# Second mixture: logits with x as the weights, a hand-written beginning with operands split from PSUM, and attention's first projection moved up

## The chip, the cores and the metric

The kernel runs on 1 core of a Trainium2 chip. The metric is the device time of one execution in microseconds (us); lower is better. The engines are PE (TensorE: matmuls, and PEld, its weight loads), DVE (VectorE), ACT (ScalarE), POOL (GpSimd) and SP (SyncE, which here issues nearly all DMAs).

## What is computed

Three stages follow one another: an attention with exponential features, a mixture of experts with one expert per token, and a second mixture in which all eight experts work on every token, weighted by a gate matrix that eight Sinkhorn-like steps balance. Everything is float32; 2304 tokens of 512 features, 8 experts of 1024 hidden units.

```python
def _attn_ref(q, k, v, w_phi):
    def phi(x):
        proj = np.einsum('bhsd,df->bhsf', x, w_phi)
        proj = proj - np.max(np.abs(proj), axis=-1, keepdims=True)
        return np.concatenate([np.exp(proj), np.exp(-proj)], axis=-1)
    ...

def _moe2_ref(x, w_gate, w1, w2):
    N, D = x.shape
    E = w_gate.shape[1]
    logits = x @ w_gate
    logits = logits - logits.max()
    P = np.exp(logits)
    for _ in range(8):
        P /= P.sum(1, keepdims=True) + 1e-09
        P /= P.sum(0, keepdims=True) + 1e-09
        P *= N / E
    out = np.zeros((N, D), dtype=np.float32)
    for e in range(E):
        h = np.maximum(x @ w1[e], 0.0)
        ye = h @ w2[e]
        out += P[:, e:e + 1] * ye
    return out
```

## The kernel before

**Attention** (`attention`, L39) runs through steps of four 128-token halves. A step has `transp` (L112: four PE transposes into one PSUM tile, copied by ACT to `th`), `proj` (L131: 8 matmuls of fp32, two row halves side by side, into the one PSUM buffer `pp`), `center` (L141: two DVE operations of 1024 columns that read `pp`) and `expo` (L148: two ACT operations). The order on PE, DVE and ACT is written out by hand (`manual_schedule`, L299); SP and POOL are left to the planner. `busy(n)` (L295) puts n transposes of the identity on PE, whose result nobody reads. At the start the order on PE is: 9 of these, the transposes of step 0, 8 more, the transposes of step 1, the projection of step 0, 16 more, and then step 1's projection.

**The first mixture** (`moe1`) ends with a scatter of its last rows to `x2d` in DRAM.

**The second mixture** (`moe2`, L816) takes the tokens in 3 passes of 2 x 384 (`h` is which 384, `TB` = 3 tiles of 128 each) and each expert's hidden units in quads of 512. Both matmuls of a quad are Strassen-like, with seven products (`mm`, L1115) instead of eight; an operand of a product is 128 x 2 x 384 (`xcb[1..7]`), as a high part (rounded to the matmul's format, by ACT, `x_high`) and a low part (the rest, by DVE, `x_low`); a product is six matmuls, high by high, high by low and low by high. Operands 1 and 2 are raw blocks of x, 6, 7, 5, 3 and 4 are sums or raw blocks (`sum_x`, `sum_4`, on DVE here). `group` (L1167) runs the seven products of 128 hidden units: `a` (PSUM `pa`) from products 1 and 2, `b` (`pb`) from 6, 5 and 3, `d` (`pd`) from 7 and 4. The copies `s`, `v`, `z` of these sums are ACT's. The `fill` functions put other work between the products: for quad 0 the transposes, the storing and the logits of the other two passes' tokens (`other_logits`, L960, four calls), later the second matmul of the quad before (`piece`).

The first three quads and all that stands before them are not written out in order. The planner takes instructions by their order in the program and by when its own model has their inputs and engine ready; in a `manual_schedule` region an engine's instructions keep the order of the program among themselves, while instructions from outside may come between. From quad 3 on everything is by hand.

The beginning (L1222 to L1245): six x tiles of 128 tokens are loaded by SP (`load_x`), each transposed on PE (four transposes into one PSUM tile, L943), and copied to `xq`, whole blocks by ACT and DVE in turn (`x_block`, L984). The operands 1 and 2 are then split from `xq`. In `group` of quad 0 the pieces `lead` stand between the two halves of `a`: `x_logits(0)`, `finish_a`, `x_logits(1)`.

`logits` (L947) has the gate weights `wg` (128 x 8 per block of 128 features) as the stationary operand and streams 384 tokens, four fp32 matmuls into an 8 x 384 tile; ACT copies that to `gt`, which has the one buffer of tag "v" in common with the copy `v`; three transposes bring 128 x 8 blocks to PSUM, and DVE copies them to `lg`. An fp32 matmul stands in the trace as two records. When all six calls are done, `sinkhorn_start` and the steps follow, in quads 0 to 2, and at their end `store_gates`.

PSUM tags: "pa" 1 buffer, "pb" 2, "pd" 1, "Y" 2, "T" 2.

Of the kernel before, what the change touches and what calls it, by code (L numbers as in the profile page):

```python
# [7 lines left out]
F32 = mybir.dt.float32  # L8
# [30 lines left out]
def attention(tc, nc, cp, q, k, v, w_phi, w_gate, w_skip, lgs, routed, stepped, early, last_steps):  # L39
# [3 lines left out]
    with ExitStack() as ctx:  # L43
# [251 lines left out]
        def busy(n):  # L295
            for _ in range(n):
                nc.tensor.transpose(warm, ident, ident)

        with tc.manual_schedule(engines={nc.tensor.engine, nc.vector.engine, nc.scalar.engine}):  # L299
            busy(9)  # L300
            th = transp(steps[0])
            busy(8)
            for g in range(len(steps) + 1):
                cur = steps[g] if g < len(steps) else []
                if cur:
                    if g:
                        t = center(proj(th))
                    else:
                        nth = transp(steps[1])
                        t = center(proj(th))  # L310
                        th = nth
                        busy(16)
                    if 0 < g < len(steps) - 1:
                        th = transp(steps[g + 1])
                    if g == 1:
                        busy(8)
# [499 lines left out]
def moe2(tc, nc, c, w_gate, w1, w2, x2d, xtd, wd1, wd2, ptd, out):  # L816
# [6 lines left out]
    with ExitStack() as ctx:  # L823
# [97 lines left out]
        def acc0(i):  # L921
            return Z[:, D * i : D * i + D]
# [16 lines left out]
        def transposed(xr, dst, copy=lambda d, s: nc.scalar.activation(d, s, AF.Copy)):  # L939

            pt = ps.tile([P, NKB, P], F32, name="pt", tag="T", bufs=2)
            for kb in range(NKB):
                nc.tensor.transpose(pt[:, kb], xr[:, kb * P : kb * P + P], c["ident"])  # L943
            for d, s in dst(pt):
                copy(d, s)

        def logits(ps_, h, src):  # L947

            pg = ps.tile([E, TW], F32, name="pg", tag="T", bufs=2)
            for kb in range(NKB):  # L950
                nc.tensor.matmul(pg, wg[:, kb], src(kb), start=(kb == 0), stop=(kb == NKB - 1))
            gt = big.tile([E, TW], F32, name="gt", tag="v")
            nc.scalar.activation(gt, pg, AF.Copy)
            pl = ps.tile([P, TB, E], F32, name="pl", tag="T", bufs=2)
            for i in range(TB):
                nc.tensor.transpose(pl[:, i], gt[:, i * P : i * P + P], c["ident"][0:E, 0:E])
            t = tiles(ps_, h)[0]
            nc.vector.tensor_copy(lg[:, t : t + TB], pl)

# [21 lines left out]
                for kh in range(2):  # L981
                    xq[h, kh] = new_xq()

        def x_block(xr, h, i):  # L984
            sl = slice(i * P, i * P + P)
            to = lambda pt: [(xq[h, kh][:, :, sl], pt[:, 2 * kh : 2 * kh + 2]) for kh in range(2)]
            if (h + i) % 2:
                transposed(xr, to, nc.vector.tensor_copy)
            else:
                transposed(xr, to)  # L990

        def x_logits(h):
            logits(0, h, lambda kb: xq[h, kb // 2][:, kb % 2])
# [132 lines left out]
        def copied(src, nm, tag):  # L1126
            t = big.tile([P, TW], F32, name=nm, tag=tag)
            nc.scalar.activation(t, src, AF.Copy)  # L1128
            return t
# [34 lines left out]
            if n == NW - 1:  # L1164
                nc.sync.dma_start(row(t, 1), accs[t])

        def group(n, g, fill, high, low, lead=()):  # L1167


            a, b, d = [ps.tile([P, TW], F32, name=nm, tag=nm, bufs=bf) for nm, bf in (("pa", 1), ("pb", 2), ("pd", 1))]  # L1170
            v = nc.vector
            mm(a, 1, g, True, False)
            s = copied(a, "s", "sz")

            def finish_a():
                mm(a, 2, g, False, True)
                relu_high(n, g, 0, 0, a)
                relu_low(n, g, 0, 0, a)

            if lead:  # L1180
                lead[0]()
                finish_a()
                lead[1]()
            mm(b, 6, g, True, False)
            high[0]()
            v.tensor_tensor(b, b, s, ALU.add)
# [2 lines left out]
            mm(d, 7, g, True, False)  # L1189
            high[1]()  # L1190
            low[1]()
            if not lead:
                finish_a()
            for k in (2, 3):
                high[k]()
                low[k]()
# [23 lines left out]

        none = lambda: None
        new_x()  # L1222
        xrs = [[load_x(t, acc0(TB * h + i)) for i, t in enumerate(tiles(0, h))] for h in range(2)]
        for h in range(2):
            for i, t in enumerate(tiles(0, h)):
                x_block(xrs[h][i], h, i)
            if h == 0:
                xs.update({1: xq[0, 0], 2: xq[0, 1]})
                for i in (1, 2):
                    x_high(i)  # L1230
                    x_low(i, True)
        for i in range(3):
            sum_x(i, True)
            if i:
                x_high(ORDER[i])
                x_low(ORDER[i])
        sum_4()
        for i in (5, 3, 4):
            x_high(i)
            x_low(i)  # L1240
        others = [(ps_, h) for ps_ in range(1, NPASS) for h in range(2)]
        load_w2(0, 0)
        load_w2(0, 1)
        for i in (6, 7, 5, 3):
            store_w1(0, i)  # L1245

        def both(*fs):
            def f():
# [4 lines left out]

        def quad(n):
            more = n + 1 < NW
            for g in range(2):
                high, low = [none] * 7, [none] * 7
                if n == 0:
# [37 lines left out]
                    low[k] = both(low[k], lambda i=i, g=g: sums_low(n, i, g))  # L1296
                if g:
                    low[0] = both(low[0], lambda: store_w2(n, 1))
                lead = [lambda: x_logits(0), lambda: x_logits(1)] if n == 0 and g == 0 else ()
                group(n, g, fill, high, low, lead)  # L1300
                if g and more:
                    if n + 2 < NW:
                        load_w1(n + 2)
# [382 lines left out]
```

## Time and profile before

| | us |
|---|---|
| median of 3 runs | 1936.58 |
| all runs | 1937.0, 1936.58, 1931.12 |
| the profiled execution | 1931.85 |
| its span, first to last instruction | 1930.1 |

| engine | busy share of the span |
|---|---|
| PE | 98% |
| PEld | 92% |
| DVE | 70% |
| ACT | 48% |
| POOL | 39% |

The shares are means over stages with different limits; what a change in one stage is worth is read from that stage. In a row of a timeline stand the start in us, the time from the first start to the last end, the engine (with q: its sequencer, which issues DMAs), the line, the operation, the tiles written and read, shapes, how often it stands in a row, and in brackets how long the engine was idle before it and what ended that. Matmuls overlap, so the time of a row is not its count times the time of one. The granted clock of PE is 1.00 for 2.4 GHz and 0.50 for 1.2 GHz.

### The profile page before, as it was taken

How to read it: one execution, taken by the hardware profiler on the slowest of the kernel's cores; microseconds unless marked ns; L12 is line 12 of the kernel's file. 1: busy time of each engine (PE TensorE's matmuls, PEld its weight loads, DVE VectorE, ACT ScalarE, POOL GpSimd, SP SyncE). 2: the span in 40 equal slices, each digit the busy share in tenths (PEclk: the TensorE clock that was granted, in tenths of full speed). 3: DMA queues.
4: the chain of work that ended last, by engine and by line, in shares of the span. 5: the costliest groups of instructions: out<-in, count | busy, mean ns of one | idle time of the engine just before them, and what ended most of it. 6: DMA issues, size and time to landing. Idle time of an engine off the chain costs nothing.

```text
span 1930.1 us, 34988 instructions
## 1 busy us (share of the span) xinstructions
PE 1887.2 (98%) x13028; PEld 1778.1 (92%) x13028; DVE 1343.9 (70%) x2309; ACT 930.8 (48%) x1679; POOL 745.9 (39%) x653
## 2 busy tenths in 40 slices
PE   9999999989999999999999999999999999999997
PEld 8998899956889988999899999999999999999997
DVE  5778977664967676767657766767786676676665
ACT  5778655545444444445344444444445444444442
POOL 2012522222433334333124455445563454444445
PEclk9999999999999999999999999999999999999999
DMA  7424686648766767777476676777656766767663
GB/s 196 119 66 164 221 281 220 211 136 288 250 219 243 254 246 245 256 267 269 140 256 224 229 237 217 237 241 251 228 174 232 237 218 232 234 223 246 227 201 110
DMA packets 234691, 422.00 MB, mean 219 GB/s; under 512 B 31594, under 2 KB 151374, under 8 KB 234508
## 3 DMA queue, kind: packets, MB, share of 16 engines
q1 hardware_dynamic: 230892, 412.16, 64.2%
q0 software_dynamic: 3456, 7.40, 1.1%
q8 instruction: 106, 1.74, 0.4%
q14 instruction: 77, 0.63, 0.1%
q10 hardware_dynamic: 160, 0.07, 0.0%
HBM read 311.18 MB, written 110.86 MB: 219 GB/s over the span
## 4 chain that ended last, share of the span: by engine, by line
PE 69%; DVE 3%; POOL 1%; DMA 1%; issue 0%; ACT 0%; POOLq 0%; DVEq 0%; ACTq 0%
PE pu L1359 23%; PE pb L1120 15%; PE py L1155 12%; PE pd L1120 10%; PE pa L1120 9%; POOL acc L1449 1%; POOL hr L1449 0%; DVE hh L1406 0%; DMA w<-wd 0%; DVE wc L884 0%; DVE xcl L1018 0%; DVE acc L1374 0%; DVE hr L1398 0%; DVE hh L1141 0%; DVE acc L1449 0%
## 5 line engine op out<-in xcount | busy, mean ns | idle before, releaser
L1359 PE MATMUL pu<-hh,w 128*128 128x384 f32 x2688 | 541.1, 336 | 8.4 <-DVE acc L1449 4.2
L1359 PEld LDWEIGHTS pu<-hh,w 128*128 128x128 f32 x2688 | 473.9, 188 | 9.4 <-DVE acc L1449 4.6
L1449 POOL TENSOR_TENSOR hr<-hr 128x384 f32<-128x384 f32 (+1 forms) x192 | 282.3, 1470 | 290.0 <-DVE hr L1398 167.6
L1120 PE MATMUL pb<-xch,wc 128*128 128x384 f32 x1152 | 297.7, 339 | 1.8 <-ACT v L1128 0.8
L1402 ACT ACTIVATE hh<-hr 128x384 fp32r<-128x384 f32 (+2 forms) x256 | 189.2, 761 | 204.6 <-POOL hr L1449 152.1
L1155 PE MATMUL py<-w,hh 128*128 128x512 f32 x1152 | 287.5, 396 | 0.0
L1406 DVE TENSOR_TENSOR hh<-hr,hh 128x384 fp32r<-128x384 f32 (+2 forms) x256 | 223.3, 881 | 63.9 <-ACT hh L1402 62.6
L1155 PEld LDWEIGHTS py<-w,hh 128*128 128x128 f32 x1152 | 215.4, 189 | 43.2 <-issue 1.9
L1372 POOL TENSOR_TENSOR acc<-acc,s 128x384 f32<-128x384 f32 x147 | 162.3, 1105 | 224.0 <-ACT s L1371 223.9
L1374 DVE TENSOR_TENSOR acc<-pu,acc 128x384 f32<-128x384 f32 x267 | 147.3, 553 | 103.9 <-PE pu L1359 103.0
L1120 PEld LDWEIGHTS pb<-xch,wc 128*128 128x128 f32 x1152 | 210.2, 188 | 9.7 <-ACT v L1128 1.7
L1120 PE MATMUL pa<-xch,wc 128*128 128x384 f32 x768 | 198.8, 338 | 0.1
L1120 PE MATMUL pd<-xch,wc 128*128 128x384 f32 x768 | 198.0, 338 | 0.5 <-DVE c L1213 0.5
L1371 ACT ACTIVATE s<-pu 128x384 f32<-128x384 f32 x147 | 72.1, 491 | 162.2 <-PE pu L1359 162.0
L1120 PE MATMUL pb<-xcl,wc 128*128 128x384 f32 x576 | 148.8, 339 | 0.0
L1120 PEld LDWEIGHTS pa<-xch,wc 128*128 128x128 f32 x768 | 139.8, 187 | 4.1 <-ACT acc L1102 0.6
L1120 PEld LDWEIGHTS pd<-xch,wc 128*128 128x128 f32 x768 | 140.0, 188 | 1.3 <-DVE c L1213 0.8
L884 DVE TENSOR_TENSOR wc<-r,wc 128x512 fp32r<-128x512 f32 x170 | 130.6, 769 | 3.8 <-ACT wc L881 3.4
L881 ACT ACTIVATE wc<-r 128x512 fp32r<-128x512 f32 x170 | 105.8, 623 | 10.6 <-PE pa L1120 9.2
L1120 PEld LDWEIGHTS pb<-xcl,wc 128*128 128x128 f32 x576 | 104.9, 188 | 0.0
L1120 PE MATMUL pa<-xcl,wc 128*128 128x384 f32 x384 | 99.1, 338 | 0.1
L1120 PE MATMUL pd<-xcl,wc 128*128 128x384 f32 x384 | 99.1, 339 | 0.0
(271 smaller groups left out, 2975.0 us busy)
## 6 DMA issues: line engine op xcount, KB each, us to landing
w<-wd SPq DMA_DIRECT2D x224, 512.0 KB, 4.2
wc<-wd SPq DMA_DIRECT2D x120, 512.0 KB, 4.9
r<-in_moe_w_dram SPq DMA_DIRECT2D x108, 512.0 KB, 4.9
wd<-wc SPq DMA_DIRECT2D x64, 512.0 KB, 3.7
wd<-acc SPq DMA_DIRECT2D x128, 256.0 KB, 3.0
wd<-w SPq DMA_DIRECT2D x96, 256.0 KB, 3.8
r<-in_moe_w_dram SPq DMA_DIRECT2D x90, 256.0 KB, 3.8
acc<-in_moe_w_dram SPq DMA_DIRECT2D x64, 256.0 KB, 3.6
```

What stands on the lines that cost most here:

```text
L881: nc.scalar.activation(wc[i][:, 0], wsrc[i], AF.Copy)
L884: nc.vector.tensor_tensor(wc[i][:, 1], wsrc[i], f32(wc[i][:, 0]), ALU.subtract)
L1120: nc.tensor.matmul(dst, wc[i][:, w, kb, sl], xcb[i][x][:, kb], start=(start and m == 0), stop=(stop and m == 5), skip_group_check=True,)
L1155: nc.tensor.matmul(py, ht[:, i * P : i * P + P], w[:, wt], start=(m == 0), stop=(m == 11))
L1359: nc.tensor.matmul(pu, w[:, wl, kb, g2 * P : g2 * P + P], H[:, hx[kb][xl].start + o], start=(m == 0), stop=(m == 5))
L1371: nc.scalar.activation(tmp, pu, AF.Copy)
L1372: nc.gpsimd.tensor_tensor(t, t, tmp, ALU.add)
L1374: nc.vector.tensor_tensor(t, pu, t, ALU.add)
L1402: nc.scalar.activation(H[:, hx[g][0]], R[:, u:v], AF.Copy)
L1406: nc.vector.tensor_tensor(H[:, hx[g][1]], R[:, u:v], f32(H[:, hx[g][0]]), ALU.subtract)
L1449: eng.tensor_tensor(out_, a, b, op)
```

## The change

Three things. `logits` makes the x blocks the stationary operand (128 x 128) and streams `wg` (8 columns), twelve fp32 matmuls per call, whose result is already tokens by experts: the copy `gt` and the transposes fall away. The beginning of the second mixture becomes `lead`, in a `manual_schedule` region over all engines: operands 1 and 2 are split straight from the transposes' PSUM tiles (`x_split`), the raw copies to `xq` follow (`x_raw`, one half by ACT, the other by DVE), and products, sums and logits have a written order; `load_w2` stands ahead of it in the program, the rest of the operands and `store_w1` (`rest_x`) behind it. In attention, step 0's projection moves ahead of step 1's transposes, with 4 warm transposes before each of them in place of 8.

```diff
@@ attention
             th = transp(steps[0])
-            busy(8)
+            busy(4)
...
                     else:
-                        nth = transp(steps[1])
                         t = center(proj(th))
-                        th = nth
+                        busy(4)
+                        th = transp(steps[1])
                         busy(16)
@@ logits
-            pg = ps.tile([E, TW], F32, name="pg", tag="T", bufs=2)
-            for kb in range(NKB):
-                nc.tensor.matmul(pg, wg[:, kb], src(kb), start=(kb == 0), stop=(kb == NKB - 1))
-            gt = big.tile([E, TW], F32, name="gt", tag="v")
-            nc.scalar.activation(gt, pg, AF.Copy)
             pl = ps.tile([P, TB, E], F32, name="pl", tag="T", bufs=2)
             for i in range(TB):
-                nc.tensor.transpose(pl[:, i], gt[:, i * P : i * P + P], c["ident"][0:E, 0:E])
+                for kb in range(NKB):
+                    nc.tensor.matmul(
+                        pl[:, i], src(kb)[:, i * P : i * P + P], wg[:, kb], start=(kb == 0), stop=(kb == NKB - 1)
+                    )
@@ x_block
+        def x_turn(xr, tag):
+            pt = ps.tile([P, NKB, P], F32, name="pt", tag=tag, bufs=2)
+            for kb in range(NKB):
+                nc.tensor.transpose(pt[:, kb], xr[:, kb * P : kb * P + P], c["ident"])
+            return pt
+
+        def x_split(pt, i):
             sl = slice(i * P, i * P + P)
...
+            for op, kh in ((1, 0), (2, 1)):
+                src = pt[:, 2 * kh : 2 * kh + 2]
+                dh, dl = [t[:, :, sl] for t in xcb[op]]
+                nc.scalar.activation(dh, src, AF.Copy)
+                nc.vector.tensor_tensor(dl, src, f32(dh), ALU.subtract)
+
+        def x_raw(pt, h, i):
+            sl = slice(i * P, i * P + P)
+            nc.scalar.activation(xq[h, 0][:, :, sl], pt[:, 0:2], AF.Copy)
+            nc.vector.tensor_copy(xq[h, 1][:, :, sl], pt[:, 2:4])
@@ group
+        def first_a(a, g):
+            mm(a, 1, g, True, False)
+            return copied(a, "s", "sz")
+
+        def finish_a(a, n, g):
+            mm(a, 2, g, False, True)
+            relu_high(n, g, 0, 0, a)
+            relu_low(n, g, 0, 0, a)
+
+        def group(n, g, fill, high, low, s=None):
+            a = None
...
+            if s is None:
+                a = ps.tile([P, TW], F32, name="pa", tag="pa", bufs=1)
+                s = first_a(a, g)
             mm(b, 6, g, True, False)
...
-            if not lead:
-                finish_a()
+            if a is not None:
+                finish_a(a, n, g)
@@ beginning
+        def lead():
+            xrs = [load_x(t, acc0(TB * h + i)) for h in range(2) for i, t in enumerate(tiles(0, h))]
+            pts = []
+            for i in range(TB):
+                pts.append(x_turn(xrs[i], "YYT"[i]))
+                x_split(pts[i], i)
+            a = ps.tile([P, TW], F32, name="pa", tag="pa", bufs=1)
+            for i in range(TB):
+                x_raw(pts[i], 0, i)
+            s = first_a(a, 0)
+            for i in range(TB):
+                pt = x_turn(xrs[TB + i], "YYT"[i])
+                x_raw(pt, 1, i)
+            finish_a(a, 0, 0)
+            sum_x(0, True)
+            sum_x(1, True)
+            x_high(6)
+            x_low(6)
+            x_logits(0)
+            sum_x(2, True)
+            x_high(7)
+            x_low(7)
+            x_logits(1)
+            return s
+
         others = [(ps_, h) for ps_ in range(1, NPASS) for h in range(2)]
         load_w2(0, 0)
         load_w2(0, 1)
-        for i in (6, 7, 5, 3):
-            store_w1(0, i)
+
+        def rest_x():
+            sum_4()
+            for i in (5, 3, 4):
+                x_high(i)
+                x_low(i)
+            for i in (6, 7, 5, 3):
+                store_w1(0, i)
@@ quad
+            s = None
+            if n == 0:
+                with tc.manual_schedule():
+                    s = lead()
+                rest_x()
...
-                lead = [lambda: x_logits(0), lambda: x_logits(1)] if n == 0 and g == 0 else ()
-                group(n, g, fill, high, low, lead)
+                group(n, g, fill, high, low, s if g == 0 else None)
```

## Rows read from the trace of the kernel before

**Rows 1.** The page: busy time, share of the span and instructions of PE.

```profile
PE 1887.2 (98%) x13028; PEld 1778.1 (92%) x13028; DVE 1343.9 (70%) x2309; ACT 930.8 (48%) x1679; POOL 745.9 (39%) x653
```

**Rows 2.** Windows: length, busy us (instructions) of PE, PEld, DVE, ACT, POOL, clock, DMA share, GB/s.

```profile
406.00:413.00 7.00, 3.42 (x14) 2.71 (x15) 0.76 (x2) 1.06 (x4) 0.00 (x0) 0.52 0.74 234
...
430.00:478.00 48.00, 44.83 (x217) 29.96 (x216) 18.72 (x36) 23.94 (x47) 11.15 (x12) 1.00 0.88 294
478.00:536.00 58.00, 54.75 (x276) 47.58 (x274) 54.51 (x133) 27.54 (x56) 22.30 (x22) 1.00 0.74 253
536.00:547.00 11.00, 8.29 (x27) 6.51 (x27) 6.42 (x11) 7.23 (x13) 4.54 (x5) 0.69 0.31 107
```

**Rows 3.** Timeline of the first 11 us: PE, ACT and DVE.

```profile
4.61 1.92 PE L297 MATMUL warm<-ident 128*128 128x128 f32 x8
4.86 0.60 ACT L123 ACTIVATE th<-pt 128x512 f32<-128x512 f32 x1 [1.31 <-PE pt L119]
7.16 1.16 PE L136 MATMUL pp<-ws,th 64*128 64x128 f32 x16
8.25 1.97 PE L297 MATMUL warm<-ident 128*128 128x128 f32 x16
8.37 1.23 DVE L143 TENSOR_REDUCE m<-pp 128x8 f32<-128x1024 f32 x1 [7.41 <-PE pp L136]
10.99 1.16 PE L136 MATMUL pp<-ws,th 64*128 64x128 f32 x16 [0.77 <-DVE t L145]
```

**Rows 4.** Timeline of PE in the second mixture's beginning.

```profile
409.39 4.58 PE L943 MATMUL pt<-ident,acc 128*128 128x128 f32 x20 [7.49 <-DMA acc<-x2d]
...
420.49 0.35 PE L956 MATMUL pl<-ident,gt 8*128 8x8 f32 x3 [0.75 <-ACT gt L953]
...
421.31 2.75 PE L951 MATMUL pg<-xq,wg 128*8 128x384 f32 x8
423.99 0.61 PE L1120 MATMUL pb<-xch,wc 128*128 128x384 f32 x2
```

**Rows 5.** Timelines of ACT and DVE in the same stretch.

```profile
411.75 0.76 DVE L945 COPY xq<-pt 128x256 f32<-128x256 f32 x2 [8.99 <-PE pt L943]
412.60 0.66 ACT L939 ACTIVATE xq<-pt 128x256 f32<-128x256 f32 x2 [1.43 <-PE pt L943]
...
419.24 0.83 ACT L1014 ACTIVATE xch<-acc 128x768 fp32r<-128x768 f32 x1
420.68 0.94 DVE L1018 TENSOR_TENSOR xcl<-acc,xch 128x768 fp32r<-128x768 f32 x1
421.55 0.95 DVE L1011 TENSOR_TENSOR t<-t,xq 128x768 f32<-128x768 f32 x1
```

**Rows 6.** Line 205 (`gate_kv`): ns shortest/median/longest; and four of its weight loads.

```profile
L205 PEld LDWEIGHTS pgk<-wgd,kvt x64: 186/192/192, 22.3 to 183.1; 128*128 128x128 f32 x64
L205 PE MATMUL pgk<-wgd,kvt x64: 183/264/285, 22.3 to 183.2; 128*128 128x18 f32 x64
...
22.26 0.52 PEld L205 LDWEIGHTS pgk<-wgd,kvt 128*128 128x128 f32 x4 [1.06 <-issue]
```

**Rows 7.** Timeline around the last logits' transposes: ACT and PE.

```profile
475.25 0.63 ACT L881 ACTIVATE wc<-s 128x512 fp32r<-128x512 f32 x1 [4.12 <-POOL s L875]
475.79 0.46 ACT L953 ACTIVATE gt<-pg 8x384 f32<-8x384 f32 x1
476.31 0.35 PE L956 MATMUL pl<-ident,gt 8*128 8x8 f32 x3 [1.37 <-ACT gt L953]
476.74 0.49 ACT L1128 ACTIVATE v<-pb 128x384 f32<-128x384 f32 x1 [0.49 <-ACT gt L953]
...
477.50 0.59 PE L1120 MATMUL pb<-xch,wc 128*128 128x384 f32 x2
```

**Rows 8.** Timeline of SP (DMA issues) at the same beginning.

```profile
406.30 3.68 SPq L936 DMA_DIRECT2D acc<-x2d  x6
410.02 0.90 SPq L1074 DMA_DIRECT2D acc<-in_moe_w_dram  x2
```

More of the change, by code (lines that the diff above doesn't have):

```diff
@@ L982, in new_x @@
                     xq[h, kh] = new_xq()
-        def x_block(xr, h, i):
-            sl = slice(i * P, i * P + P)
[L986 to L990, printed above, removed]
+        def x_turn(xr, tag):
[4 more added lines that the diff above has]
+        def x_split(pt, i):
+            sl = slice(i * P, i * P + P)
+            for op, kh in ((1, 0), (2, 1)):
[7 more added lines that the diff above has]
+            nc.vector.tensor_copy(xq[h, 1][:, :, sl], pt[:, 2:4])
         def x_logits(h):
@@ L1165, in piece @@
                 nc.sync.dma_start(row(t, 1), accs[t])
-        def group(n, g, fill, high, low, lead=()):
-            a, b, d = [ps.tile([P, TW], F32, name=nm, tag=nm, bufs=bf) for nm, bf in (("pa", 1), ("pb", 2), ("pd", 1))]
-            v = nc.vector
[L1172 to L1181, printed above, removed]
-                finish_a()
-                lead[1]()
+        def first_a(a, g):
[7 more added lines that the diff above has]
+            a = None
+            b, d = [ps.tile([P, TW], F32, name=nm, tag=nm, bufs=bf) for nm, bf in (("pb", 2), ("pd", 1))]
+            v = nc.vector
+            if s is None:
+                a = ps.tile([P, TW], F32, name="pa", tag="pa", bufs=1)
+                s = first_a(a, g)
             mm(b, 6, g, True, False)
@@ L1191, in group @@
             low[1]()
-            if not lead:
-                finish_a()
+            if a is not None:
+                finish_a(a, n, g)
             for k in (2, 3):
@@ L1222, in moe2 @@
         new_x()
[L1223 to L1240, printed above, removed]
+        def lead():
[22 more added lines that the diff above has]
+            return s
         others = [(ps_, h) for ps_ in range(1, NPASS) for h in range(2)]
```

## Prediction

> **What bounds the kernel now.** I read the page's engine line first: PE has work for 98% of the span [rows 1]. A change is therefore worth what it takes out of PE's stream, or out of a gap in it; faster copies elsewhere are worth nothing by themselves. Next came the windows by stage, since the diff touches only three places [rows 2]. From 406 to 413 us PE works 3.42 of 7 us at a granted clock of 0.52, that is mostly at 1.2 GHz: the second mixture's x rows arrive after the first mixture's scatter. From 430 to 478 PE has small gaps while the DMA engines are 0.88 busy. From 478 to 536 VectorE (DVE) is busy 54.51 of 58 us with the Sinkhorn steps; this stretch begins when the last logits are there. From 536 to 547 the clock is down again (0.69). Then come the timelines: the first 11 us [rows 3], the second mixture's beginning on PE [rows 4] and on ACT and DVE [rows 5], and the last logits [rows 7].
>
> **Attention's beginning.** Before, PE runs T0 (transposes of step 0), 8 warm transposes, T1, and only then the projection, at 7.16 us; its input th0 was copied by 4.86 + 0.60 = 5.46 us [rows 3]. After, 4 warm transposes stand between. The 8 take 1.92 us, thus start (1.92 - 0.42) / 7 = 0.21 us apart (the low clock; the 16 later ones are 0.11 apart), so 4 end their issue at 4.61 + 0.85 = 5.46, and the projection can start at about 5.6. What comes next is half its speed: spacing changes near 6.9 us before (16 projection matmuls take 1.16 us at 7.16). I leave that moment where it is. Eight pairs then take six steps of 0.21 and two of 0.11, and `center` on DVE starts at about 7.35 instead of 8.37: 1.0 us earlier. If the clock comes up late the gain is 0.85; if at once, 1.5. T1 is now behind: projection to 7.1, 4 warm (0.44), T1 (0.44), 16 warm (1.75): PE is through at 9.75, before `t` is ready at about 9.9 (10.85 - 1.0). The number of warm transposes is 24 either way. T1 issues no load, and th1's copy still stands between th0's and `expo` on ACT; SP and POOL have nothing moved. The second projection waits for DVE [rows 3], so the 1.0 us carries on; after it attention is a stream of PE. I take **-1.0** (0 to -1.5: at 0 a later load ends last instead).
>
> **The logits, six calls.** Removed per call: 4 fp32 matmuls of 384 columns, which are 8 records in 2.75 us (0.32 apart; 2.68 to the next matmul), ACT's `gt` copy, and 3 small transposes (0.35 us) [rows 4]. On PE that is about 3.05 us. Added: 12 fp32 matmuls, 24 records, each a 128x128 weight load with 8 columns streamed. Nearest row: `gate_kv`, fp32, 128x128 weights, 18 columns: 4 weight loads in 0.52 us, and one takes 0.19, so they are 0.11 us apart [rows 6]. 24 x 0.11 = 2.65, plus 0.1 at the change of shape: 2.75. So **-0.3 a call**; the weight load sets the pace, not the columns. Bounds: if half of each load were hidden, -1.6 a call; if each record waited for the end of the one before, 0.26 each [rows 6], +3.3. I take 0.11, as that row has the same weights and nearly the same stream. Four calls lie in quad 0's fillers: -1.2. The two of the beginning are counted below.
>
> The copy `gt` also leaves a wait. At the last call PE idles 1.37 us: `gt` runs at 475.79, held on ACT by the w1 copy, which had waited for POOL [rows 7]. After the change PE goes from logits to pieces. But ACT's `v` copy waits behind the same w1 copy and now starts at 475.85 instead of 476.74; PE needs it for the pb matmuls at 477.50. So the next thing late is `v`, and I count **-1.0** (0 to -1.4). The other waits on `gt` of this kind are small, except the first (0.75), which is in the next part.
>
> **The second mixture's beginning.** T0 to T2 are unchanged: rows land one by one and the clock is low, and ACT can read the third block at 412.60 [rows 5]. Before, the blocks are copied, then the 384-wide operands are split, and after the logits `pb` starts at 423.99 [rows 4]; one `pl` is still to come then, whose issue is about 0.2 us of its 0.35. After, each block gets two high halves (ACT), two low halves (DVE) and a raw copy on each; two copies of that size take 0.66 us on ACT and 0.76 on DVE [rows 5], one about 0.4. Reading only by data, `xch1` is whole at 412.9, its low part at 413.4, `first_a` is issued by 414.25, and T3 starts there. If instead ACT and DVE take turns on a PSUM tile, each low part delays the next high part: the third block's lows end near 413.9 and 414.7, DVE's first raw copy at 415.0, T3 at 415.1. From T3 on PE has 12 transposes (1.3), `finish_a` (1.1) and 48 logit records (5.3): 7.7 us. So `pb` at 422.8 or 421.95, against 423.99 + 0.2. No row shows the two engines in one tile at once: before, ACT and DVE alternate by whole blocks [rows 5]. I therefore take the dearer: **-1.4** (-2.3 with overlap; 0 if DVE is late, below).
>
> The Trainium skill ("PSUM — Partial Sum Buffer", section "PSUM bank collisions raise a hardware error") says that ScalarE and VectorE may not read one bank's same partitions at once and that the program must order them. By it the beginning gives 1.4, without it 2.3; no row here bears on it.
>
> What hides DVE: `relu_low` now stands ahead of `sum_x(0)` in DVE's hand-written order and waits for `finish_a` (about 417.5), so the five sums and lows queued behind wait too. Start at 418.7, two sums (0.87 each, spacing of [rows 5]), x_high 0.83, x_low 0.87: operand 6 is whole at 422.2, 0.6 us ahead of PE. If that cover is gone by more than 2 us, the gain of this part is gone. Operand 7 is whole at 424.9, and `pd` waits about 1 us unless the planner puts the next tiles' transposes there. `load_w2` stands before the x loads in the program now: before, it is behind them on SP [rows 8]. If it runs while SP waits for the scatter it costs nothing; if it runs at 406.3, two issues of 0.45 us delay the x rows by 0.9 to 1.
>
> **Sum.** -1.0 - 1.2 - 1.0 - 1.4 = -4.6 us. The profiled execution took 1931.85 us (span 1930.1): **1927.2**. That execution is near the fastest run shown; the median is 4.7 us above it, so a median at the same levels would be up to 1932.
>
> **Rivals.** (a) The stretch 430 to 478 is bound by transfers (0.88 share, 294 GB/s), and logits that cost less only wait longer for x rows and w1: the -1.2 and -1.0 are lost: 1929.4. For: the share; POOL, which held the w1 copy, itself works on loaded weights. Against: PE has work 44.83 of 48 us.
> (b) More than the sum: ACT and DVE overlap (-0.9), and the idle stretch around `store_gates` (536 to 547 us: PE 8.29 us busy, clock 0.69 [rows 2]) keeps the clock up this time, as the planner's order of quads 0 to 2 is new: another -3.4 (11 x 0.31). 1922.9. For: that order is planned anew. Against: the wait is for DVE, which is as loaded as before.
> (c) Slower: during the logits the clock falls. No row shows 48 weight loads in a row with 8 columns each. At the low clock their 0.11 becomes 0.21: 144 x 0.1 = +14.4; with -3.4 from the rest, 1942.9. It decides from 0.143 us a record (0.111 + 4.6 / 144). Against: attention's narrow matmuls run at full clock.
> (d) The change does nothing that lasts: the planner gives back what the beginning gains, by waits for DVE in the 478 to 536 stretch: 1930.9, attention's 1.0 alone.
>
> **How the numbers follow.** Chances: forecast 0.41, (a) 0.18, (b) 0.22, (c) 0.09, (d) 0.10. A measurement of this kernel can tell about 0.3%, 5.8 us, from no change. The forecast, with its terms at their larger ends (1.5 + 1.2 + 1.4 + 2.3, and whatever of the calls overlaps), reaches to 6.4 us and more; I put some two fifths of it beyond 5.8. Faster: these and (b): 0.40. Slower: (c) and a little of (d): 0.11. Within: 0.49. The range goes from 1920 ((b) with the larger attention gain and logits) to 1935.5 (the sum on the upper level of the runs, or most of it lost there); (c) and the far end of (b) are left out.
>
> **What would show it.** Right: `center` first at 7.3 to 7.5 us; logit records 0.11 apart; no wait on `gt`; `pb` of the second mixture about 13.4 us after the first x transpose (before 14.6), less when ACT and DVE overlap. Wrong: the second projection still at 11 us; records 0.2 apart; PE waiting for DVE at `pb` or `pd` for over 1.5 us; a new stretch at low clock; the first x transpose over 3.1 us (406.30 to 409.39) after the first x load [rows 4, 8].

## The result, and the profile after

The changed kernel takes 1943.91 us (median of 6 executions, 1941.57 to 1944.64) against 1934.88 of the kernel before: ratio 1.0055, 95% interval 1.0041 to 1.0069. It is slower, by 9.0 us between the medians and by some 10.6 by the ratio (it is not the quotient of the two medians, which is 1.0047). The forecast was 1927.2, and the range ended at 1935.5. The profiled execution of after has 1944.5 us, its span 1942.8, which is 12.7 more than before; the rows below are from it.

The page, with PE's busy time (compare [rows 1]): the share fell by one point, and PE is busy 5.9 us longer.

```profile
PE 1893.1 (97%) x13106; PEld 1798.9 (93%) x13106; DVE 1349.3 (69%) x2313; ACT 929.7 (48%) x1677; POOL 746.5 (38%) x653
```

Windows of the second mixture's stage, first of before, then of after (length, busy us of PE, PEld, DVE, ACT, POOL, granted clock, DMA share, GB/s), and behind it the rest of the quads, where PE is full in both:

```profile
403.00:560.00 157.00, 140.37 (x674) 108.64 (x675) 105.91 (x217) 78.12 (x152) 45.42 (x46) 0.96 0.70 234
560.00:980.00 420.00, 419.44 (x2085) 377.50 (x2084) 292.66 (x460) 190.17 (x370) 143.95 (x145) 1.00 0.69 239
```

```profile
403.00:560.00 157.00, 132.80 (x686) 117.71 (x687) 99.48 (x206) 70.35 (x138) 42.67 (x43) 0.88 0.64 213
560.00:980.00 420.00, 419.43 (x2084) 377.40 (x2083) 296.92 (x465) 194.43 (x377) 145.31 (x147) 1.00 0.69 241
```

So the loss lies between 403 and 560 us (PE ends the first mixture only 0.8 us later than before): PE idles 7.6 us more there, and the clock's mean is 0.08 lower, which over 157 us is 12.6 us of full speed. (Some of the idle time is at the low clock, so the two don't add up.) Finer windows of after show where the clock is at 1.2 GHz; [rows 2] had 0.52 from 406 to 413 and 1.00 from 430 to 536:

```profile
413.00:424.00 11.00, 7.65 (x32) 6.34 (x31) 6.45 (x15) 6.57 (x17) 3.92 (x6) 0.66 0.85 287
424.00:434.20 10.20, 10.20 (x50) 10.20 (x49) 3.76 (x5) 1.31 (x3) 2.05 (x2) 0.50 0.51 166
434.20:439.00 4.80, 4.80 (x14) 3.85 (x14) 0.83 (x1) 2.23 (x4) 0.00 (x0) 0.50 0.01 2
439.00:449.20 10.20, 9.29 (x63) 8.23 (x63) 8.43 (x16) 5.94 (x11) 0.00 (x0) 1.00 0.41 118
449.20:452.70 3.50, 3.50 (x14) 3.41 (x13) 2.03 (x4) 1.40 (x3) 0.00 (x0) 0.51 0.85 332
```

From 424 to 439 PE has work every moment, and still runs at half clock. The timeline of PE in after tells with what (it answers to [rows 4]; in brackets the idle time ahead and what ended it):

```profile
411.76 1.94 PE L985 MATMUL pt<-ident,acc 128*128 128x128 f32 x8 [9.06 <-DMA acc<-x2d]
...
416.35 0.62 PE L1129 MATMUL pa<-xch,wc 128*128 128x384 f32 x2 [1.31 <-ACT xch L993]
...
419.65 2.79 PE L985 MATMUL pt<-ident,acc 128*128 128x128 f32 x12 [1.82 <-issue]
...
424.16 10.24 PE L952 MATMUL pl<-wg,xq 128*128 128x8 f32 x48
...
446.11 2.85 PE L952 MATMUL pl<-wg,acc 128*128 128x8 f32 x24
...
554.85 0.83 PE L1129 MATMUL pb<-xch,wc 128*128 128x384 f32 x2 [3.38 <-ACT v L1137]
```

The 48 logit records of the beginning take 10.24 us, 0.21 apart; 24 of a later call, at full clock, take 2.85, as forecast (2.75), and right behind them the clock falls again (449.2). The three other later calls run at 0.11 as well, and no fall follows them. The first x transpose starts at 411.76 instead of 409.39. SP shows one reason, as w2 now stands ahead of x (compare [rows 8]), and ACT shows another, copies of w2 (L1088) that wait for their DMA between the beginning's own (L993; compare [rows 5]):

```profile
406.74 1.70 SPq L1083 DMA_DIRECT2D acc<-in_moe_w_dram  x2
408.48 2.80 SPq L936 DMA_DIRECT2D acc<-x2d  x6
```

```profile
413.81 0.66 ACT L993 ACTIVATE xch<-pt 128x256 fp32r<-128x256 f32 x2 [0.49 <-DVE xcl L994]
...
417.52 0.63 ACT L1088 ACTIVATE w<-acc 128x512 fp32r<-128x512 f32 x1 [1.23 <-DMA acc<-in_moe_w_dram]
418.06 0.36 ACT L993 ACTIVATE xch<-pt 128x256 fp32r<-128x256 f32 x1
```

Two theories follow. **Theory 1**: matmuls that stream 8 columns behind each 128x128 weight load bring TensorE's clock down, or keep it there. **Theory 2**: the gaps of the new beginning (1.31 and 1.82 us, the late x rows) do that, and the logits only run in their shadow. Apart from both, the order of SP's queue and the attention part have prices of their own.

### The profile page after: what moved, and what is told of

Same layout as the page of the kernel before. It is cut to its first block, busy times and chain, and to the rows that moved or that the text cites. A ratio compares the mean times of both kernels' runs of the same rounds, so it can differ in the third digit from the quotient of the medians.

```text
span 1942.8 us, 35147 instructions
## 1 busy us (share of the span) xinstructions
PE 1893.1 (97%) x13106; PEld 1798.9 (93%) x13106; DVE 1349.3 (69%) x2313; ACT 929.7 (48%) x1677; POOL 746.5 (38%) x653
## 4 chain that ended last, share of the span: by engine, by line
PE 71%; DVE 4%; POOL 1%; DMA 1%; ACT 1%; issue 1%; SPq 0%; POOLq 0%; ACTq 0%; DVEq 0%
PE pu L1387 22%; PE pb L1129 15%; PE py L1164 13%; PE pd L1129 10%; PE pa L1129 10%; PE pl L952 1%; POOL acc L1477 1%; POOL hr L1477 0%; DVE hh L1434 0%; DVE xcl L1027 0%; DMA wd<-acc 0%; DVE wc L884 0%; PE pt L943 0%; DMA w<-wd 0%; DVE acc L1402 0%
```

## The experiments

Ratios are to the kernel before, run on the same chip, each with its 95% interval. They differ from the quotients of the medians by up to 0.0008. The clock is the mean over the profiled execution, which is not always a typical one: it is the slowest of eleven for pad128, the second slowest of eleven for fill_pad and the fastest of twelve for w2late_pad. Each 0.001 of the clock is 1.9 us of full speed.

| kernel | ratio | clock |
|---|---|---|
| before | 1 | 0.993 |
| after | 1.0055 (1.0041 to 1.0069) | 0.987 |
| before + new logits (logonly) | 1.0067 (1.0051 to 1.0084) | 0.986 |
| before + new logits, 128 columns (logonly_pad) | 0.9990 (0.9980 to 1.0000) | 0.993 |
| the same, 128 columns in the two early calls only (lead_pad) | 1.0019 (1.0010 to 1.0028) | 0.988 |
| the same, 128 columns in the four later calls only (fill_pad) | 1.0012 (1.0001 to 1.0023) | 0.988 |
| after, logits with 128 columns (pad128) | 1.0003 (0.9994 to 1.0012) | 0.989 |
| after, old logits (widelog) | 1.0037 (1.0024 to 1.0050) | 0.990 |
| after, w2 loads late (w2late) | 1.0029 (1.0018 to 1.0041) | 0.987 |
| after, w2 late, old logits (w2late_wide) | 1.0000 (0.9988 to 1.0012) | 0.993 |
| after, w2 late, 128 columns (w2late_pad) | 1.0009 (0.9999 to 1.0019) | 0.993 |
| before + w2 loads early (w2early) | 1.0016 (1.0007 to 1.0025) | 0.990 |
| before + attention part (attnonly) | 0.9999 (0.9990 to 1.0008) | 0.993 |
| before + attention part + logits, 128 columns (attn_pad) | 0.9996 (0.9987 to 1.0005) | 0.994 |

**The logits in the changed kernel (pad128, widelog).** pad128 streams wg sixteen times over and uses the first 8 columns:

```diff
-            pl = ps.tile([P, TB, E], F32, name="pl", tag="T", bufs=2)
+            pl = ps.tile([P, TB, 16, E], F32, name="pl", tag="T", bufs=2)
...
-                        pl[:, i], src(kb)[:, i * P : i * P + P], wg[:, kb], start=(kb == 0), stop=(kb == NKB - 1)
+                        pl[:, i], src(kb)[:, i * P : i * P + P], wg[:, kb].unsqueeze(1).to_broadcast([P, 16, E]),
+                        start=(kb == 0), stop=(kb == NKB - 1)
...
-            nc.vector.tensor_copy(lg[:, t : t + TB], pl)
+            nc.vector.tensor_copy(lg[:, t : t + TB], pl[:, :, 0])
```

> The changed kernel, but each logits matmul streams the 8 columns of wg sixteen times over (128 columns, the same weight load, one bank written instead of 96 bytes; the first 8 columns are used, so the output stays the same). At full clock the transposes of 128x128 stand 0.10 to 0.11 us apart, as the narrow records do, so the padding itself should cost next to nothing there. Theory 1 (the narrow records keep the clock down): the clock rises some 7 us after the lead's last gap ends (419.7), so by about 427; the 48 records of the lead take 6 to 7 us instead of 10.24, the wide work behind them runs at full clock (2.4 us less) and the second fall at 449.3 is gone (1.7 us less): about 7 to 8 us less, 1936 to 1937 us. Theory 2 (the gaps ahead of the logits bring the clock down and hold it there): the clock stays at half until about 439 as before the edit; the time stays within 1 us of 1943.9.

Measured: 1.0003, some 10 us under after, where I had said 7 to 8. Nearly all of the loss is gone, although the beginning is untouched: 9.51 us of idle time ahead of the first x transpose (after: 9.06) and the same gap of 1.31. The timeline of PE and three windows of pad128:

```profile
417.28 1.01 PE L1130 MATMUL pa<-xch,wc 128*128 128x384 f32 x2 [1.31 <-ACT xch L994]
...
420.69 2.79 PE L986 MATMUL pt<-ident,acc 128*128 128x128 f32 x12 [1.12 <-issue]
...
425.20 5.86 PE L952 MATMUL pl<-wg,xq 128*128 128x128 f32 x48
```

```profile
420.70:425.90 5.20, 5.20 (x22) 5.20 (x23) 3.75 (x8) 3.25 (x8) 1.46 (x2) 0.50 0.89 285
425.90:437.00 11.10, 11.10 (x85) 10.74 (x85) 10.87 (x16) 7.20 (x13) 2.78 (x2) 1.00 0.56 166
437.00:450.00 13.00, 12.41 (x95) 11.99 (x94) 7.09 (x15) 7.35 (x16) 0.00 (x0) 1.00 0.91 275
```

The clock comes back early in the 48 records, at 425.9 and so 5.2 us after the last gap (I had said 7), they take 5.86 us instead of 10.24, and there is no fall near 449. Sixteen times the columns cost nothing, since the weight load sets the pace.

widelog puts the old `logits` (wg as weights, 384 columns streamed, the copy `gt`, narrow transposes) into the changed kernel.

> The changed kernel with the logits of the kernel before (wg as weights, 384 columns streamed, a copy and narrow transposes behind them); the hand-written beginning and the attention part stay. Theory 1 (narrow records keep the clock down): the clock comes back during or right after the logits, before 430, and no fall at 449; about 6 to 9 us less than the changed kernel, 1935 to 1938 us. Theory 2 (gaps of the new beginning hold it down): half clock until about 439, and 1942 to 1944 us.

Measured: 1.0037, 0.0018 less than after; on the scale of after's median 1940.4. Theory 1's prediction for the clock holds:

```profile
423.41 3.39 PE L951 MATMUL pg<-xq,wg 128*8 128x384 f32 x8
```

```profile
405.00:424.50 19.50, 10.82 (x38) 8.62 (x39) 9.06 (x19) 8.73 (x21) 4.27 (x6) 0.50 0.79 248
424.80:450.00 25.20, 24.80 (x125) 16.68 (x123) 18.12 (x28) 15.07 (x28) 4.26 (x3) 1.00 0.73 235
```

Its time was a miss: I had said 1935 to 1938 us. With the old logits the new beginning costs more than I allowed (see the queue order below).

**The logits alone (logonly, logonly_pad).** Here the beginning, the queues and attention are those of before; only `logits` is new, with 8 columns in the one and with the padding of pad128 in the other. So nothing of theory 2 stands ahead of them.

> The kernel before with the new logits alone (x as weights, 8 columns of wg streamed); beginning and attention as before, so there are no new gaps ahead of the logits, and the clock is up when they begin. Theory 1 (narrow records bring the clock down): the clock falls within the lead's 48 records, the later of them are 0.21 us apart; 3 to 8 us slower than before, ratio 1.0015 to 1.004. Theory 2 (only the gaps of the new beginning bring it down): the records stay at 0.11 us and the time falls by my forecast's two terms for the logits, 1.2 + 1.0 us: ratio 0.999. My forecast says 0.999.

> The kernel before with the new logits alone, each matmul streaming 128 columns. Theory 1: the clock stays up through the lead's 48 records at 0.11 us each, and what is left is the saving that I forecast for the logits (1.2 + 1.0 us): ratio 0.999. If the form itself brings no saving even at full clock: 1.000. If something else than the number of columns makes this form slow: as with 8 columns, 1.0015 to 1.004.

Measured: 1.0067 and 0.9990. One number in the code decides about 15 us. First the timeline of PE and four windows of logonly, then the same timeline and one window of logonly_pad:

```profile
417.05 2.74 PE L952 MATMUL pl<-wg,xq 128*128 128x8 f32 x24
...
420.80 3.99 PE L952 MATMUL pl<-wg,xq 128*128 128x8 f32 x24
```

```profile
417.00:422.00 5.00, 5.00 (x44) 5.00 (x42) 4.75 (x7) 3.71 (x7) 3.25 (x3) 1.00 0.00 2
422.00:429.00 7.00, 7.00 (x29) 6.81 (x29) 4.99 (x8) 1.68 (x3) 0.00 (x0) 0.51 0.15 41
...
480.30:487.00 6.70, 6.70 (x23) 5.58 (x23) 2.08 (x7) 2.19 (x5) 1.18 (x1) 0.51 0.79 249
493.80:497.20 3.40, 3.40 (x10) 2.72 (x9) 3.40 (x9) 1.72 (x4) 0.46 (x1) 0.51 1.02 343
```

```profile
419.12 2.84 PE L952 MATMUL pl<-wg,xq 128*128 128x128 f32 x24
...
422.86 2.84 PE L952 MATMUL pl<-wg,xq 128*128 128x128 f32 x24
```

```profile
422.00:429.00 7.00, 6.58 (x46) 5.84 (x45) 6.79 (x9) 4.21 (x7) 0.23 (x1) 1.00 0.25 75
```

In logonly the first call runs at full clock, 24 records in 2.74 us; the clock falls at 422 in the second (3.99 us), with PE busy 5.00 of 5.00 us ahead of it, and the wide work behind runs at half speed until 429. With 128 columns both calls take 2.84. The planner's order on PE is the same in the two kernels up to the end of the second call, so the fall there is no matter of another order; behind it the orders differ. Nor is it a matter of one execution: the mean clock is 0.985 or 0.986 in all six of logonly, and 0.991 to 0.994 in all twelve of logonly_pad. Theory 2 is out as the only cause, and theory 1 is shown. What the runs do not show is how the 15 us divide: the last of the later calls brings the clock down too (480.3), but the low stretch at 493.8 has no logits ahead of it, only a wait of 2.07 us for DVE, and so belongs to the Sinkhorn stretch as it was planned there. The 0.9990 also is what my two terms for the logits had said (1.2 + 1.0 us), though the interval only just keeps 1.

**Early and late calls (lead_pad, fill_pad).** `n` is 16 or 1 by pass; the lines of lead_pad against logonly_pad (fill_pad has `16 if ps_ else 1`):

```diff
+            n = 16 if ps_ == 0 else 1
...
-                        pl[:, i], src(kb)[:, i * P : i * P + P], wg[:, kb].unsqueeze(1).to_broadcast([P, 16, E]),
+                        pl[:, i, 0:n], src(kb)[:, i * P : i * P + P], wg[:, kb].unsqueeze(1).to_broadcast([P, n, E]),
```

> The kernel before with the new logits, where the 48 records of the two calls at the stage's start stream 128 columns and the 96 of the four later calls stream 8 (the output stays the same). It splits the loss of the new logits alone (1.0067 with 8 columns, 0.999 with 128) between early and late calls. If the loss goes by number of records, a third of it is healed: 1.004. If only records that stand in runs of 24 and 48 without wide work between them bring the clock down, and the later calls are split by the filler's order, nearly all of it is healed: 0.999 to 1.001.

> The kernel before with the new logits, where the 48 records of the two calls at the stage's start stream 8 columns and the 96 of the four later calls stream 128. If the loss goes by number of records, two thirds are healed: 1.0015. If the start carries it: 1.005 to 1.0065, with the clock down from about 422 to 429 us as in the run of the logits alone.

Measured: 1.0019 and 1.0012. lead_pad lies between the two lines that I had drawn, fill_pad near the count by records. Either group of calls alone brings the clock down. The fourteen traces agree: from 432 to 475 us, where the later calls lie, the mean clock is 1.00 in the ten kernels whose later calls are wide or padded, and 0.88 to 0.96 in the four where they stream 8 columns (after, logonly, lead_pad, w2late; in after the tail of the early calls, to 439, is in it). A window of fill_pad behind its early calls, and one of lead_pad in the fillers:

```profile
425.30:432.00 6.70, 6.70 (x26) 6.51 (x27) 4.56 (x8) 1.44 (x2) 0.00 (x0) 0.50 0.16 42
```

```profile
432.00:438.70 6.70, 6.70 (x24) 6.70 (x25) 2.37 (x5) 1.00 (x3) 1.08 (x2) 0.50 0.70 226
```

Over 0.9990 the early calls cost 0.0022, the late ones 0.0029, both together 0.0077. The whole is more than the sum by 0.0026, about as much as the four intervals leave open together; why, I can't say.

**The queue order (w2early, w2late, w2late_wide, w2late_pad).** w2early moves one thing in the kernel before; the three others move it back in the changed one (with the old logits, or with 128 columns):

```diff
         new_x()
+        load_w2(0, 0)
+        load_w2(0, 1)
         xrs = [[load_x(t, acc0(TB * h + i)) for i, t in enumerate(tiles(0, h))] for h in range(2)]
...
-        load_w2(0, 0)
-        load_w2(0, 1)
```

```diff
-        load_w2(0, 0)
-        load_w2(0, 1)
...
                 with tc.manual_schedule():
                     s = lead()
+                load_w2(0, 0)
+                load_w2(0, 1)
                 rest_x()
```

> The kernel before with one thing of the changed kernel: the two w2 loads stand ahead of the loads of x on SP's queue. If the queue order costs what the first x transpose shows (1.55 us of delay): ratio 1.0008. If it also puts the w2 copies of ACT, which wait for their DMA, ahead of the copies out of PSUM, as in the changed kernel: up to the difference between the two kernels with the old logits (1.0037 and 1.0000): 1.0035. If the planner holds the order of before anyway: 1.0000.

> The changed kernel with the loads of w2 issued behind the hand-written beginning, so that the x rows stand first on SP's queue (1.55 us of the 2.37 us by which the first x transpose is late) and no w2 operation of ACT that waits for a DMA can stand between the beginning's own. Theory 1 (narrow records): the x transposes start 1.5 us sooner and the gaps of 1.31 and 1.82 us shrink, but the 48 records of the logits are still 0.21 us apart at half clock: 1.5 to 3.5 us less, 1940.4 to 1942.4 us. Theory 2 (gaps): without the gaps the clock, once up at about 415, stays up, and the 48 records stand 0.11 us apart: 8 to 10 us less, 1934 to 1936 us.

> The changed kernel with the logits of the kernel before and the w2 loads behind the beginning: what is left of the change is the hand-written beginning and the attention part. My forecast for these two alone: 1.4 + 1.0 us less, ratio 0.9988. Theory of the queue order: the x transposes start within 0.3 us of the kernel before (w2 late did that), so the 1.55 us of the w2 loads are gone, and the clock is up by about 418: ratio 0.999 to 1.000. Rival: the beginning keeps its cost (operands split from PSUM in turns of ACT and DVE, work pushed into the gate's stretch, where more gaps then stand): 1.0015 to 1.003, little better than the changed kernel with the old logits alone (1.0037).

> The changed kernel with both mends: the w2 loads behind the hand-written beginning, and each logits matmul streaming 128 columns (the 8 of wg sixteen times; the output stays the same). Theory 1 plus the queue order: with the w2 loads late the clock came up ahead of the logits and fell under the second 24 narrow records; with 128 columns it should stay up, the 48 records of the lead should take some 5.2 us (0.11 apart) instead of 8.2, and the wide work behind them run at full clock: some 5 to 6 us less than with the w2 loads late alone (ratio 1.0029), so 0.9995 to 1.0005 of the kernel before. If the two mends take the same time away (each heals what the other does), no better than 128 columns alone: 1.0003 and above. My forecast for the whole change, had its terms held, was 0.9976.

Measured: w2early 1.0016, that is 3.1 us (1.4 to 4.8), about twice the delay of 1.55 us, though the interval still takes that in. Its x transposes start after 9.43 us of idle time, where [rows 4] has 7.49, so the delay itself is 1.94 here:

```profile
406.96 2.15 SPq L1074 DMA_DIRECT2D acc<-in_moe_w_dram  x2
409.15 2.81 SPq L936 DMA_DIRECT2D acc<-x2d  x6
```

```profile
412.32 1.09 PE L943 MATMUL pt<-ident,acc 128*128 128x128 f32 x4 [9.43 <-DMA acc<-x2d]
```

w2late: 1.0029, some 5 us under after. It is between the two theories' times, and its trace tells them apart, as PE has one gap over 0.4 us between the x transposes and the end of the logits (0.82, at 413), and the clock is up when the logits begin:

```profile
415.42 2.60 PE L985 MATMUL pt<-ident,acc 128*128 128x128 f32 x12
...
418.92 3.10 PE L952 MATMUL pl<-wg,xq 128*128 128x8 f32 x24
...
422.44 5.12 PE L952 MATMUL pl<-wg,xq 128*128 128x8 f32 x24
```

```profile
418.00:421.20 3.20, 3.20 (x28) 3.20 (x27) 2.61 (x6) 2.96 (x6) 0.99 (x1) 0.99 0.74 189
421.20:431.40 10.20, 10.20 (x41) 9.72 (x41) 3.58 (x5) 2.74 (x4) 1.45 (x2) 0.50 0.36 123
```

The clock falls with the narrow records running and PE never idle. In after, the clock had fallen inside the gap of 1.82; here it falls without one, under narrow records.

w2late_wide: 1.0000. With the w2 loads behind the beginning and the old logits, the new beginning and the attention part are neither gain nor loss that can be seen. Against widelog (1.0037) the queue order is worth 0.0037, far more than 1.55 us. In widelog's trace the ACT copies of w2 hold up the third x block as in after, and the clock stays at half until 424.5; what each of the two weighs was not separated. Nor has the queue order one price: with 8 columns it is worth 0.0026 (after and w2late), with 128 columns nothing that can be seen (1.0003 and 1.0009), although pad128's trace has the same late x rows and the same w2 copies on ACT. Why the old logits pay most for it stays open.

w2late_pad: 1.0009, no better than pad128 (1.0003), against what I expected of both mends together. The intervals overlap, and by the medians alone the order is the other way round (1.0005 and 1.0011). In the profiled execution the beginning is in order, as PE's timeline and a window show, but that is the fastest of the twelve (1930.57 us, against a median of 1933.34) and one of three with a mean clock of 0.993; the other nine have 0.990 to 0.992, and what is slower in them no trace shows.

```profile
416.18 2.44 PE L986 MATMUL pt<-ident,acc 128*128 128x128 f32 x12
...
419.49 5.52 PE L952 MATMUL pl<-wg,xq 128*128 128x128 f32 x48
```

```profile
418.40:440.00 21.60, 20.36 (x144) 18.56 (x142) 17.25 (x29) 13.75 (x26) 5.12 (x6) 1.00 0.75 226
```

**The attention part (attnonly, attn_pad).** attnonly takes that hunk of the diff alone; attn_pad adds the logits with 128 columns.

> The kernel before with the attention part of the change alone. In the changed kernel's trace the second projection came 1.6 us sooner, 0.5 us of it was left from the fourth step to the 187th us, and four gaps on PE with no releaser at 189.5 to 191.7 turned that into 0.7 us late. If these gaps are an accident of where the changed program's instructions lie, this kernel keeps the 0.5 us: 1934.4 us, ratio 0.9997. If they come with the attention part itself: 0.7 us slower, 1935.6 us, ratio 1.0004. My forecast's own step said 1.0 us less: 1933.9 us. The three differ in the trace at the start of the first mixture (196.87 us in the kernel before), hardly in the time.

> The kernel before with the attention part and the new logits at 128 columns, without the hand-written beginning and the queue order that comes with it: what of the change should be worth keeping. The logits so (0.9990) and the attention part (0.9999) were each measured alone: 0.9989 if they add up, and under 1.0000 in any case. If the attention part's 0.5 us is real and lasts, 0.9985.

Measured: 0.9999 and 0.9996. PE's timeline of attnonly, then of attn_pad, at the second and third projection:

```profile
9.96 1.16 PE L136 MATMUL pp<-ws,th 64*128 64x128 f32 x16
...
16.74 0.41 PE L119 MATMUL pt<-ident,qt 128*128 128x128 f32 x2 [0.69 <-DMA qt<-in_q_dram]
```

```profile
9.40 1.16 PE L136 MATMUL pp<-ws,th 64*128 64x128 f32 x16
...
17.07 0.41 PE L119 MATMUL pt<-ident,qt 128*128 128x128 f32 x2 [1.39 <-DMA qt<-in_q_dram]
```

The second projection comes 1.0 and 1.6 us sooner than in [rows 3]. That trace is a late one: in the five other kernels with the attention of before the second projection starts at 10.13 to 10.60 us, in the eight with the new one at 9.14 to 9.96, on the mean 1.0 us sooner. At 16 to 17 us PE waits for q's DMA, which no one has moved. Whatever was gained up to there is handed back: this transpose starts at 16.09 to 17.07 us in the eight, after a wait in each, and at 16.93 in the kernel before, without one. attn_pad's 0.9996 is no gain over logonly_pad, and its interval holds my 0.9989. The gaps of PE that I had noticed in after (four, 1.41 us in all; the third is shown) are in neither of these two kernels; logonly, which has no attention part, shows four of them (1.52 us). So they don't belong to this part, and what makes them stays open:

```profile
190.99 0.23 PE L228 MATMUL po<-kvf,fq 128*64 128x74 f32 x1 [0.36 <-issue]
```

None of the kernels is faster than before by more than can be told; logonly_pad is nearest to it. Nor do the prices add up: the new logits alone cost 0.0067, the rest of the change with the old logits 0.0037 (widelog), and the whole 0.0055.

## Why the prediction was wrong

- **The logits' term: the step that failed.** I took the spacing of `gate_kv` [rows 6], 0.11 us, for all 144 records, as the weights and nearly the stream are the same. That spacing was right at full clock (2.74 and 2.85 us for 24), and so was the reason given for it: 128 columns take 2.84. The price was wrong because the clock did not stay up: in logonly, where the new logits stand alone, my two terms for them (1.2 and 1.0 us less) came out as 13 us more (1.0067), and in after `pb` starts 27.2 us after the first x transpose, where 13.4 was to be the sign of a right forecast. What I did not carry over is that `gate_kv` stands in fours between other work, and these records in 24 and 48. I had this as rival (c), at 0.09. The evidence against it, that attention's narrow matmuls run at full clock, was of another pattern. The right inference would have been that no row bounds it, and a much larger chance.
- **Rival (c)'s size fits by accident.** 144 x 0.1 less 3.4 gave 1942.9. In the trace only the 48 early records stand 0.21 apart in full (10.24 us against the 5.52 of w2late_pad: 4.7 us); the four later calls ran at 0.11. The rest of the loss is wide work that follows at half clock (434.2 to 439, 449.2 to 452.7), the later x rows, and more idle time up to 560 us. With 128 columns in the kernel before, the logits save what the two terms said: 2.2 us forecast, 1.9 measured (0.9990; 0 to 3.9).
- **`load_w2` ahead of x.** I named it, priced it at 0.9 to 1 if it ran at 406.3, and then counted it at nothing. It ran at 406.74, took 1.70 us of SP's queue, and alone costs 1.0016, about 3 us (1.4 to 4.8). In after SP waits ahead of the w2 loads, at last for the DMA of the scatter to `x2d`, so there was no earlier time in which they could have run for nothing. [rows 8] could not show that, as w2 stands behind x there; with the question open, the price that I had named belonged in the sum.
- **The beginning: -1.4, measured about 0.** The turns of ACT and DVE on a PSUM tile that I took for the sum are there (ACT waits 0.49 for DVE's `xcl`). The Trainium skill ("PSUM — Partial Sum Buffer", section "PSUM bank collisions raise a hardware error") says the program must order the two engines; the trace agrees, and the overlap of -0.9 was rightly left out. Two things were missing. The planner puts other operations between the hand-written ones on ACT, and one of them, waiting for w2, holds up those behind it: 1.23 us in after, and then a gap of 1.82 on PE (the profile names no releaser for that gap; the order of the rows on ACT and DVE suggests it). And I left the rise of the clock where it was. In w2late_pad, which has neither the late x rows nor that wait, T3 starts at 416.18, 6.1 us after the first x transpose (I had 5.7), at half clock until about 418; before, the clock was at full by 413. That eats the rest: `pb` comes 15.0 us after the first x transpose, against 14.6 before and my 13.4. With the beginning of before and the same padded logits in it the three other traces have 13.5 to 14.1 (attn_pad, lead_pad, logonly_pad), so in the traces the hand-written beginning is some 1 us later, where I had it 1.4 earlier.
- **Attention: -1.0, measured 0.** The step itself was right: `center` starts at 6.70 us, which is 1.67 sooner than in [rows 3], but over all traces at 6.49 to 7.31 with the new attention (eight) and at 7.50 to 8.37 with the old (six), 1.0 us sooner on the mean. The rest of the 1.67 is the moment at which the clock comes up, which differs from trace to trace with the same code (the 16 projection records take 1.17 us in after and 1.76 in attnonly). The bound of 0 that I gave ("a later load ends last instead") is what happened: the q transpose of the third step waits for its DMA. In the kernel before, that transpose began without a wait, so nothing in its timeline showed how close the load was behind (in fill_pad, with the attention of before, it waits 1.51 us).
- **The wait on `gt`** is gone, as said. At the stage's end PE still waits 3.38 us for ACT's `v` (before: 0.77 at the same place), and the Sinkhorn stretch has more gaps, eight of 0.4 to 1.5 us. The four kernels whose later calls stream 8 columns wait 2.8 to 3.6 us for `v` there, the ten others at most 2.5 (logonly_pad 1.17), so the wait goes with the narrow records. How much of the other gaps comes from the new logits and how much from a planner whose order is new each time, no run here separates.
- **The clock without a gap.** The Trainium skill ("TensorE: Matmul & The Clock Gate", section "HAM oscillation — how this bites in real kernels") tells of a clock that falls because bursts of matmuls wait for DMA between them. In after the fall at 418.6 did come in such a gap (1.82 us, though not one that a DMA ended), but in w2late and logonly the clock fell with PE busy throughout, so waits were not the only case to look for here.

## What to carry to other kernels

Before turning a wide matmul round so that a narrow operand streams, look for a row with the same stream in as long a run, and read its granted clock; a spacing from four records does not tell at which clock forty-eight will run. Where the weight load sets the pace, repeating the streamed operand costs nothing in time and can keep the clock. And a block written out by hand is still only as early as the queues ahead of it, so read where its loads land on SP and which foreign operations the planner may place between its own.

## What the runs showed of the hardware

- TensorE went from 2.4 to 1.2 GHz while it had work without a break, in fp32 matmuls of 8 columns behind 128x128 weight loads (w2late: busy 3.20 of 3.20 us at 0.99, then 10.20 of 10.20 at 0.50); the same matmuls with 128 columns held 1.00 (w2late_pad, 418.4 to 440). Not every such run brings it down: behind three of the four later calls of after it stayed at 1.00.
- The clock's level reaches beyond the instructions that set it: wide matmuls that follow take about twice their time until it is back (after: 434.2 to 439, clock 0.50, all busy).
- 24 fp32 records with 128 columns take 2.84 us, with 8 columns 2.74 to 2.85. With the clock at half the 48 with 8 columns take 10.24.
- Four of the fourteen profiled executions show gaps on PE with no releaser, 0.9 to 1.7 us in all, at 189 to 192 us in the same unchanged loop (L228); w2late_pad has two, 0.35 with none and 0.39 put down to "remote".
